# Two of the first query/key loads wait for a used buffer, and three more loads change places in the queue

## Chip, cores and metric

One NeuronCore of a Trainium2 chip (trn2). The time is that of one execution on the device, in microseconds (us); of several executions the median is given.

## What is computed

Attention with 4 batches, 8 heads, 576 positions and a head size of 64, in two parts that are added, followed by two mixer layers on the result. All data is float32 for q, k, v; the mixers' weights are 64-bit floats that the kernel itself converts.

```python
q_d, k_d, v_d = (t.reshape(B, H, Sd, 4, D).mean(axis=3) for t in (q, k, v))     # pooled by 4: 144 positions
out_up = np.repeat(sm_attn(q_d, k_d, v_d), 4, axis=2)                           # full softmax attention, repeated
mask = np.abs(pos[:, None] - pos[None, :]) < 4                                  # local: 7 neighbours
out_local = np.matmul(softmax(where(mask, q @ k.T / 8, -1e9)), v)
x = (out_up + out_local)                                                        # then as [B, S, 512]
u = x + (relu(x.T @ w_tok1) @ w_tok2).T;  x = u + relu(u @ w_ch1) @ w_ch2       # first mixer
th = x @ w_theta;  y = w_tok_r @ (x * cos(th)) + w_tok_i @ (x * sin(th))        # second mixer
u = x + y;  result = u + relu(u @ w_ch)
```

## The kernel before

The work is cut into small generators, one per step and tile, and a table `ORDER` (L33) lists by name which generator runs on next; each entry emits the instructions up to the generator's next `yield`. So the table sets the order of the instructions on every engine, and the engines then wait for one another by semaphores. What bears on the change lies in the first 100 us, the attention.

Heads are handled in 16 *pairs* (two heads of one batch; pairs 0 to 3 are batch 0, pairs 4 to 7 batch 1, and a tile `qk_1_3` is pair 7). For a pair n the steps are:

- `Pn` (`load_pair`, L375): one load of q and k of the pair, 128 partitions x 1164 values, 582 KB, into a tile `qk`. Four buffers exist; the pool gives each new tile one whose last reader is known.
- `Wn` (`load_values`, L382): four loads of the values `vw` (two of 32 rows, two of 6).
- `Kn` (`pool_pair`, L413): two additions on VectorE (L421, L422) that pool q and k by 4.
- `Ln` (`pair_local`, L522): local attention. 12 matmuls on zeros (24 for pair 0; L315) keep TensorE running, then the scores (L533, which read `qk`), a maximum and a subtraction on VectorE (L545, L546), the exponential on ScalarE (L553), transposes (L558), copies (L561), the product with `vw` (L568), and a division (L577 to L582). A pair's `qk` buffer is free when its L421 and its L533 have run.
- `An` (L590) adds the pooled part.

Two pairs make a quad Q. `VQ` (`pool_values`, L391) loads `vd` (650 KB) and pools it on GpSimd. `FQ` (`quad_front`, L425) is the pooled attention: scores (L434, L443), maxima (L452, L460), exponentials (L468, L473), transposes, the product `od` (L493 to L500), the division `ods` (L504 to L507), a store of `ods` to DRAM (L510, L511; the "store" below), and three loads `xu` of it, repeated (L516, L519; the "pooled loads"). `TQ`, `EQ`, `UQ` are the token mixer. `G0` to `G6` load and convert blocks of the token mixer's weights, `X0`, `X1`, ... those of the channel mixer: a load `raw` (L187), two operations on ScalarE (L199, L201), three on VectorE (L203, L206, L215), one on GpSimd (L219), a cast and a subtraction (L221, L223). `raw_2` and `raw_3` are blocks of `w_tok1` (512 KB), `raw_0`, `raw_4`, `raw_5` and `raw_6` of `w_tok2` (288 KB).

All these loads and stores are issued by SyncE (SP), one after the other in the order of the table; SP stops at one whose buffer is not free yet, and all behind it wait too. The framework gives the loads eight semaphores in turn (`DMAHW0` to `DMAHW7`), so that a load is also not issued before the load eight places ahead of it has landed.

The buffer of a pair's load, before:

```python
qk = sb2.tile([128, 2, S + 6], F32, tag="qk", name=f"qk_{b}_{p4}", bufs=4)   # L377
sp.dma_start(qk, qkT[b, p4])                                                 # L378
```

Of the kernel before, what the change touches and what calls it, by code (L numbers as in the profile page):

```python
# [12 lines left out]
F32 = mybir.dt.float32  # L13
# [101 lines left out]
def kernel(  # L115
# [172 lines left out]
    sb1 = actx.enter_context(tc.tile_pool(name="a1", bufs=1))  # L288
    sb2 = actx.enter_context(tc.tile_pool(name="a2", bufs=2))
# [3 lines left out]
    def wide(name):  # L293
        return big.tile([128, 2, 512], F32, tag="big", name=name)
# [25 lines left out]
    def step(name, gen):  # L320
        gens[name] = gen
# [200 lines left out]
    def pair_local(n):  # L522
# [426 lines left out]
    def lazily(f):  # L949
        yield from f()  # L950
# [190 lines left out]
    sb1 = ctx.enter_context(tc.tile_pool(name="c1p", reuse_waits="tile", bufs=1))  # L1141
    sb2 = ctx.enter_context(tc.tile_pool(name="c2p", reuse_waits="tile", bufs=2))
# [93 lines left out]
    T0, T1 = slice(0, HALF), slice(HALF, S)  # L1236
# [221 lines left out]
```

## Time and profile before

| | before |
|---|---|
| median of 3 runs | 682.81 us (680.63 to 683.04) |
| profiled execution | 679.18 us, its span 677.4 us |
| TensorE (PE) busy | 655.6 us, 97% |
| weight loads (PEld) busy | 625.6 us, 92% |
| VectorE (DVE) busy | 519.8 us, 77% |
| ScalarE (ACT) busy | 321.1 us, 47% |
| GpSimd (POOL) busy | 100.1 us, 15% |
| bytes moved by DMA | 109.93 MB, mean 162 GB/s |

The profile is of one execution; its rows are times in us from the start of the span. Busy shares are averages over stages with different limits. A row of a timeline names the engine, the source line, the operation, the tile written and the tiles read; in brackets stands how long the engine had been idle before it and what it waited for.

### The profile page before, as it was taken

What the parts mean: (1) busy time and instruction counts of PE and PEld (TensorE: products, weight loads), DVE (VectorE), ACT (ScalarE), POOL (GpSimd) and SP (SyncE); (2) the same over time, 40 slices, a digit from 0 to 9 for tenths busy, and PEclk for the clock granted to TensorE, in tenths of its full rate; (3) what the DMA queues carried; (4) which work ended last, traced back from release to release, by engine and by line L of the source; (5) the groups of instructions that cost most, each with busy time, mean ns of one, the idle gap of its engine ahead of it and who ended that gap; (6) DMA issues with size and microseconds to landing.
All of it is one profiled execution on the core that took longest, in us unless ns stands there. A gap on an engine that the chain in (4) does not pass through costs nothing.

```text
span 677.4 us, 17394 instructions
## 1 busy us (share of the span) xinstructions
PE 655.6 (97%) x7320; PEld 625.6 (92%) x7320; DVE 519.8 (77%) x952; ACT 321.1 (47%) x632; POOL 100.1 (15%) x92
## 2 busy tenths in 40 slices
PE   7779889999999999999999999999999999999997
PEld 4658879989999999999999999999999998998997
DVE  5989988697542888998987867677898748847837
ACT  3566758355342564535434523154647227427311
POOL 3224222415000423300101200012000000000000
PEclk8889999999999999999999999999999999999999
DMA  8797877757343685527263762699510330140202
GB/s 294 235 300 236 269 248 250 254 184 233 105 147 126 221 294 187 202 65 214 57 195 128 206 142 85 236 323 277 141 63 0 106 121 1 62 142 1 71 1 70
DMA packets 93021, 109.93 MB, mean 162 GB/s; under 512 B 46880, under 2 KB 69536, under 8 KB 92944
## 3 DMA queue, kind: packets, MB, share of 16 engines
q1 hardware_dynamic: 92080, 106.08, 49.4%
q0 software_dynamic: 864, 2.75, 1.1%
q8 instruction: 57, 0.93, 0.6%
q14 instruction: 20, 0.16, 0.1%
HBM read 79.13 MB, written 29.69 MB: 161 GB/s over the span
## 4 chain that ended last, share of the span: by engine, by line
PE 84%; DMA 5%; DVE 5%; SPq 2%; ACT 2%; issue 1%; DVEq 0%; ACTq 0%
PE y L157 6%; PE y L158 6%; PE y L159 6%; PE c L158 4%; PE c L157 4%; PE c L159 4%; PE c L699 4%; PE c L702 4%; PE c L700 4%; PE c_p L902 3%; PE c_p L905 3%; PE c_p L903 3%; PE th L158 2%; PE th L159 2%; PE th L157 2%; DMA qk<-qkT 2%
## 5 line engine op out<-in xcount | busy, mean ns | idle before, releaser
L158 PE MATMUL y<-wrl,zh 128*128 128x288 f32 x256 | 74.9, 296 | 0.0
L157 PE MATMUL y<-wrh,zh 128*128 128x288 f32 x256 | 74.8, 296 | 0.0
L159 PE MATMUL y<-wrh,zl 128*128 128x288 f32 x256 | 71.9, 295 | 0.0
L219 POOL TENSOR_TENSOR ww<-ww,raw 128x512 int32<-128x512 int32 (+2 forms) x30 | 41.0, 1373 | 160.1 <-DMA raw<-w_ch 52.9
L157 PEld LDWEIGHTS y<-wrh,zh 128*128 128x128 f32 x256 | 48.0, 188 | 0.0
L158 PEld LDWEIGHTS y<-wrl,zh 128*128 128x128 f32 x256 | 48.0, 188 | 0.0
L159 PEld LDWEIGHTS y<-wrh,zl 128*128 128x128 f32 x256 | 46.9, 188 | 0.0
L219 POOL TENSOR_TENSOR raw<-raw 128x512 int32<-128x512 int32 (+2 forms) x16 | 20.4, 1275 | 133.5 <-DVE raw L215 57.6
L1231 DVE TENSOR_TENSOR cx<-y,cx 128x288 f32<-128x288 f32 x32 | 14.6, 456 | 32.3 <-PE y L159 31.8
L151 ACT CAST cuh<-cx 128x288 fp32r<-128x288 f32 (+1 forms) x16 | 8.8, 553 | 59.6 <-DVE cx L1231 59.6
L199 ACT ACTIVATE ww<-raw 128x512 f32<-128x512 f32 (+2 forms) x30 | 19.5, 649 | 27.4 <-DVE c1l L223 9.5
L157 PE MATMUL th<-thh,cxh 128*128 128x512 f32 (+1 forms) x92 | 31.6, 343 | 0.0
L158 PE MATMUL th<-thl,cxh 128*128 128x512 f32 (+1 forms) x92 | 31.6, 343 | 0.0
L159 PE MATMUL th<-thh,cxl 128*128 128x512 f32 (+1 forms) x92 | 31.1, 343 | 0.0
L921 DVE SCALAR_TENSOR_TENSOR g<-c,g 128x384 fp32r<-128x384 f32 x40 | 21.1, 549 | 12.8 <-ACT g L918 12.8
L918 ACT ACTIVATE g<-c 128x384 fp32r<-128x384 f32 x40 | 19.2, 490 | 24.4 <-PE c L159 24.4
L201 ACT ACTIVATE raw<-raw 128x512 int32<-128x512 uint32 (+3 forms) x46 | 29.5, 641 | 0.0
L929 DVE TENSOR_TENSOR ut<-c,ut 128x384 f32<-128x384 f32 x32 | 17.1, 550 | 9.9 <-PE c L702 9.9
L568 PE MATMUL o<-vw,plt 38*32 38x65 f32 x1280 | 18.0, 231 | 3.8 <-issue 3.1
L157 PE MATMUL t<-w2h,h 128*128 128x256 f32 (+1 forms) x64 | 21.5, 337 | 0.0
L157 PE MATMUL c<-uh,c1h 128*128 128x384 f32 x64 | 21.4, 334 | 0.0
L159 PE MATMUL c<-uh,c1l 128*128 128x384 f32 x64 | 21.4, 334 | 0.0
(390 smaller groups left out, 2256.7 us busy)
## 6 DMA issues: line engine op xcount, KB each, us to landing
raw<-w_ch SPq DMA_DIRECT2D x27, 512.0 KB
qk<-qkT SPq DMA_DIRECT2D x16, 582.0 KB
xT<-ut SPq DMA_DIRECT2D x12, 768.0 KB
vd<-vtok SPq DMA_DIRECT2D x8, 650.0 KB
vw<-vloc SPq DMA_DIRECT2D x32, 146.2 KB
uT<-us SPq DMA_DIRECT2D x16, 288.0 KB
ut<-uT SPq DMA_DIRECT2D x6, 768.0 KB
ut<-xT SPq DMA_DIRECT2D x6, 768.0 KB
```

The lines of the kernel that those rows point to most:

```text
L157: pe.matmul(out, lh, rh, start=start, stop=False, skip_group_check=again)
L158: pe.matmul(out, lh, rl, start=False, stop=False, skip_group_check=again)
L159: pe.matmul(out, ll, rh, start=False, stop=stop, skip_group_check=again)
L201: act.activation(f, words[:, :, 0], AF.Copy, scale=2.0**-29)
L219: pool.tensor_tensor(out=w.bitcast(I32), in0=w.bitcast(I32), in1=f, op=ALU.add)
L699: pe.matmul(ps[:, 0:MIX], h[:, cb % 2, d], h1, start=cb == cbs[0], stop=False)
L700: pe.matmul(ps[:, 0:MIX], l[:, cb % 2, d], h1, start=False, stop=False)
L702: pe.matmul(ps[:, 0:MIX], weight[cb // 2][2][:, cb % 2, d], h2, start=False, stop=cb == cbs[-1])
L902: pe.matmul(ps[:, 0:MIX], h[:, cb % 2, d], h1, start=cb == cbs[0], stop=False)
L903: pe.matmul(ps[:, 0:MIX], l[:, cb % 2, d], h1, start=False, stop=False)
L905: pe.matmul(ps[:, 0:MIX], weight[cb // 2][2][:, cb % 2, d], h2, start=False, stop=cb == cbs[-1])
L921: dve.scalar_tensor_tensor(out=h2, in0=ps, scalar=0.0, in1=h1.bitcast(F32), op0=ALU.max, op1=ALU.subtract)
```

## The change

The table of the order is rewritten in its first four lines, and the buffer of each pair's load is set by hand.

```diff
 ORDER = """
-G3 P0 G2 I*2 P1 G3 P4 G3 V0 P2 G3 K0 G3 G2 I G2 I L0*2 P3 K1 F0 W1 L0 F0 L1 L0 G3 F0 V0 L1*2 V0 L2 W0 G1 G0 G6 V1 G2
-K2 V0 G2 F0 L1 F0 L2 K3 K4 L0 F0 L0 L2 L1 G2 F1 L2 L1 L0 F0 F1 G1*2 F1 V1 F0 P5 F0 W3 L0 F1 G5 G0 L1 G0 F1 K5 G6 F2 L1
...
+G3 P0 G2 I*2 P1 G3*2 V0 G3 K0 G3 G2 I G2 I L0*2 P2 W0 G1 K1 F0 L0 F0 L1 L0 G3 F0 V0 L1 P3 G0 W1 L1 V0 L2 G2 K2 V0 G2
+F0 G1 L1 F0 L2 G1 K3 L0 F0 L0 L2 F1 L1 G2 L2 L1 L0 F0 F1*2 F0 V1 P4 P5 F0 V1 G6 W3 L0 F1 G5 G0 L1 G0 F1 K4 K5 G6 F2 L1
...
+QK = (0, 1, 0, 1, 2, 3, 0, 1, 3, 2, 3, 0, 2, 1, 3, 0)
...
-        qk = sb2.tile([128, 2, S + 6], F32, tag="qk", name=f"qk_{b}_{p4}", bufs=4)
+        qk = sb1.tile([128, 2, S + 6], F32, tag=f"qk{QK[n]}", name=f"qk_{b}_{p4}")
```

Pair 2 now loads into pair 0's buffer and pair 3 into pair 1's; pairs 4 and 5 have buffers of their own and are loaded behind the first store; from pair 6 on each load takes the buffer of the same earlier pair as before. The added line moves the line numbers of the changed kernel up by one. The amount of work and the number of instructions stay the same; TensorE's order changes in one place (the scores of quad 1's second half, L434 and L443, now come before the transposes of pair 1, L558), and behind about 60 us all engines have the order of before.

SP, the first loads. The names are `qk` of a batch and pair, `vd` of a batch and quad, `vw` values, `raw` weights; in brackets the semaphores that the load waits for. Before:

```order
L378 DMA qk_0_1_148<-qkT 128x1164
L378 DMA qk_1_0_152<-qkT 128x1164
L396 DMA vd_0_0_157<-vtok 128x1300
L378 DMA qk_0_2_159<-qkT 128x1164 [waits DMAHW0_49]
L378 DMA qk_0_3_240<-qkT 128x1164 [waits DMAHW1_49,DVE_49,PE_49]
L387 DMA vw_0_1_266<-vloc 32x1170 [waits DMAHW2_49]
```

Now:

```order
L379 DMA qk_0_1_148<-qkT 128x1164
L397 DMA vd_0_0_155<-vtok 128x1300
L379 DMA qk_0_2_236<-qkT 128x1164 [waits DMAHW1_49,DVE_49,PE_49]
L388 DMA vw_0_0_238<-vloc 32x1170 [waits DMAHW0_49]
L388 DMA vw_0_0_238<-vloc 32x1170
L388 DMA vw_0_0_238<-vloc 6x1170 [waits DMAHW2_49]
L388 DMA vw_0_0_238<-vloc 6x1170 [waits DMAHW3_49]
L188 DMA raw_2_243<-w_tok1 128x2x256 [waits DMAHW4_49]
L379 DMA qk_0_3_342<-qkT 128x1164 [waits DMAHW5_49,DVE_49,PE_49]
```

Pair 4 (`qk_1_0`) is gone from the head of the queue, pair 2 stands where pair 3 stood and waits for the same readers of pair 0, and pair 3 has moved behind `vw_0_0` and `raw_2` and waits for the readers of pair 1.

SP, around the first store (`od`, `ot`) and the pooled loads (`xu`). Before:

```order
L187 DMA raw_4_373<-w_tok2 128x288 [waits DMAHW4_49]
L396 DMA vd_0_1_375<-vtok 128x1300 [waits DMAHW5_49,Pool_49]
L510 DMA od_0_0_57<-ods_0_0_567 4x32x256 [waits DMAHW6_49,DVE_49]
L511 DMA ot_0_0_65<-ods_0_0_567 4x32x64 [waits DMAHW7_49]
L378 DMA qk_1_1_589<-qkT 128x1164 [waits DMAHW0_49,PE_49]
L516 DMA xu_0_0_591<-od_0_0_57 128x1x1024 [waits DMAHW6_49,DMAHW1_49]
L519 DMA xu_0_0_591<-ot_0_0_65 64x1x256 [waits DMAHW7_49,DMAHW2_49]
L519 DMA xu_0_0_591<-ot_0_0_65 64x1x256 [waits DMAHW3_49]
L387 DMA vw_0_3_595<-vloc 32x1170 [waits DMAHW4_49,PE_49]
```

Now:

```order
L511 DMA od_0_0_57<-ods_0_0_562 4x32x256 [waits DMAHW3_49,DVE_49]
L512 DMA ot_0_0_65<-ods_0_0_562 4x32x64 [waits DMAHW4_49]
L397 DMA vd_0_1_578<-vtok 128x1300 [waits DMAHW5_49,Pool_49]
L379 DMA qk_1_0_580<-qkT 128x1164 [waits DMAHW6_49]
L379 DMA qk_1_1_582<-qkT 128x1164 [waits DMAHW7_49]
L517 DMA xu_0_0_584<-od_0_0_57 128x1x1024 [waits DMAHW3_49,DMAHW0_49]
L520 DMA xu_0_0_584<-ot_0_0_65 64x1x256 [waits DMAHW4_49,DMAHW1_49]
L520 DMA xu_0_0_584<-ot_0_0_65 64x1x256 [waits DMAHW2_49]
L188 DMA raw_4_589<-w_tok2 128x288
L388 DMA vw_0_3_591<-vloc 32x1170 [waits PE_49]
```

`vd_0_1` and `raw_4` were issued ahead of the store and now come behind it, and both pairs 4 and 5 stand between the store and the pooled loads. Further on, at the second store (`od_0_1`), pair 7's load moves in the same way: it stood ahead of the store and stands behind the three `xu` loads of it now, and so does `vd_1_0`; the weights `raw_7` and `raw_8` of the channel mixer swap places.

DVE, the pooling of pairs 2 to 4 (`qa`, `qkd`), the conversion of `raw_2`, and the maximum of pair 2 (`mx_0_2`). Before:

```order
L546 TENSOR_TENSOR pbuf1_120<-s_0_1_278,mx_0_1_344 128x2x5x38
L421 TENSOR_TENSOR qa_0_2_379<-qk_0_2_159 128x576
L422 TENSOR_TENSOR qkd_0_1_378<-qa_0_2_379 128x288
L421 TENSOR_TENSOR qa_0_3_443<-qk_0_3_240 128x576
L422 TENSOR_TENSOR qkd_0_1_378<-qa_0_3_443 128x288
L421 TENSOR_TENSOR qa_1_0_447<-qk_1_0_152 128x576
L422 TENSOR_TENSOR qkd_1_0_446<-qa_1_0_447 128x288
L545 TENSOR_REDUCE mx_0_2_488<-s_0_2_349 128x10
```

Now:

```order
L547 TENSOR_TENSOR pbuf1_120<-s_0_1_276,mx_0_1_351 128x2x5x38
L422 TENSOR_TENSOR qa_0_2_373<-qk_0_2_236 128x576
L423 TENSOR_TENSOR qkd_0_1_372<-qa_0_2_373 128x288
L204 TENSOR_SCALAR raw_2_243<-raw_2_243 128x512
L207 TENSOR_SCALAR raw_2_243<-raw_2_243 128x512
L216 SCALAR_TENSOR_TENSOR raw_2_243<-raw_2_243 128x512
L422 TENSOR_TENSOR qa_0_3_442<-qk_0_3_342 128x576
L423 TENSOR_TENSOR qkd_0_1_372<-qa_0_3_442 128x288
L546 TENSOR_REDUCE mx_0_2_483<-s_0_2_356 128x10
```

The conversion of `raw_2` stood seven places behind `mx_0_2` and now stands ahead of pair 3's pooling; pair 4's pooling has left this place for one behind `raw_3`'s conversion, just ahead of pair 5's.

## Rows read from the trace of the kernel before

**Rows 1.** Busy time by stretches of the span; the first line names the columns.
```profile
core 0: us, PE busy (x) PEld busy (x) DVE busy (x) ACT busy (x) POOL busy (x), PEclk, DMA share, GB/s
0.00:9.54 9.54, 6.48 (x126) 4.06 (x126) 3.71 (x10) 3.44 (x7) 2.56 (x8) 1.00 0.81 279
10.90:14.10 3.20, 3.20 (x29) 1.78 (x29) 2.87 (x6) 1.17 (x4) 1.41 (x2) 0.50 1.10 393
...
19.00:24.00 5.00, 4.70 (x201) 3.77 (x187) 3.96 (x11) 3.45 (x9) 0.00 (x0) 1.00 1.02 371
24.00:35.09 11.09, 7.92 (x254) 5.72 (x252) 10.62 (x23) 5.63 (x16) 5.95 (x6) 0.85 0.66 215
...
38.00:45.00 7.00, 3.64 (x170) 2.89 (x172) 6.11 (x11) 6.20 (x14) 0.00 (x0) 1.00 0.89 297
100.00:160.00 60.00, 59.00 (x1108) 54.08 (x1109) 50.58 (x94) 37.17 (x88) 17.20 (x20) 1.00 0.70 229
```

**Rows 2.** Chain that ended last, in order of time: start, us, what.
```profile
3.53 5.99 DMA qk<-qkT
...
42.99 1.85 issue
...
127.51 7.42 DMA qk<-qkT
```

**Rows 3.** Timeline of VectorE: start, us, line, tiles, count, [idle before, releaser].
```profile
5.63 1.19 DVE L421 TENSOR_TENSOR qa<-qk 128x576 f32<-128x576 f32 x1 [0.37 <-DMA qk<-qkT]
...
7.88 0.43 DVE L215 SCALAR_TENSOR_TENSOR raw<-raw 128x256 uint32<-128x256 uint32 x1
...
15.92 0.55 DVE L545 TENSOR_REDUCE mx<-s 128x10 f32<-128x380 f32 x1 [1.65 <-PE s L533]
...
19.54 0.76 DVE L421 TENSOR_TENSOR qa<-qk 128x576 f32<-128x576 f32 x1
...
20.71 0.55 DVE L545 TENSOR_REDUCE mx<-s 128x10 f32<-128x380 f32 x1
...
25.15 0.43 DVE L203 TENSOR_SCALAR raw<-raw 128x512 f32<-128x512 f32 x1
...
26.07 0.69 DVE L215 SCALAR_TENSOR_TENSOR raw<-raw 128x512 uint32<-128x512 uint32 x1
...
48.52 0.83 DVE L421 TENSOR_TENSOR qa<-qk 128x576 f32<-128x576 f32 x1
```

**Rows 4.** Timeline of ScalarE, the conversion of raw_5.
```profile
35.09 0.48 ACT L199 ACTIVATE ww<-raw 128x288 f32<-128x288 f32 x1 [4.25 <-DMA raw<-w_tok]
```

**Rows 5.** Timeline of SP, the issuing queue.
```profile
1.20 0.42 SPq L378 DMA_DIRECT2D qk<-qkT  x1
...
8.81 0.33 SPq L378 DMA_DIRECT2D qk<-qkT  x1
...
24.41 0.44 SPq L378 DMA_DIRECT2D qk<-qkT  x1
...
43.53 0.60 SPq L516 DMA_DIRECT2D xu<-od  x1
```

**Rows 6.** Timeline of TensorE, the matmuls on zeros of pairs 1 and 2.
```profile
11.99 2.89 PE L315 MATMUL s<-zero 128*128 128x320 bf16 x12
...
15.82 1.80 PE L315 MATMUL s<-zero 128*128 128x320 bf16 x12
```

**Rows 7.** DMA issues: tiles, queue, count, KB of each.
```profile
qk<-qkT SPq DMA_DIRECT2D x16, 582.0 KB
...
vd<-vtok SPq DMA_DIRECT2D x8, 650.0 KB
vw<-vloc SPq DMA_DIRECT2D x32, 146.2 KB
...
xu<-od SPq DMA_DIRECT2D x8, 512.0 KB
...
raw<-w_tok SPq DMA_DIRECT2D x4, 288.0 KB
```

More of the change, by code (lines that the diff above doesn't have):

```diff
@@ L33 @@
 ORDER = """
-G3 P0 G2 I*2 P1 G3 P4 G3 V0 P2 G3 K0 G3 G2 I G2 I L0*2 P3 K1 F0 W1 L0 F0 L1 L0 G3 F0 V0 L1*2 V0 L2 W0 G1 G0 G6 V1 G2
-K2 V0 G2 F0 L1 F0 L2 K3 K4 L0 F0 L0 L2 L1 G2 F1 L2 L1 L0 F0 F1 G1*2 F1 V1 F0 P5 F0 W3 L0 F1 G5 G0 L1 G0 F1 K5 G6 F2 L1
-G0 P6 W2 G5 G6 L3 V1 F2 V1 L3 G6 F2 F1 L3 G1 G4 F1 L2 P7 L5 L2 L5 F1 G1 L3 A0 V2 X0 A1 T0 L3 G1 L5 G0 L3 T0 G0 L2 G2
-F1 G4 F2 G5 T0 K6 T0 V2 X2 L2 G6 W5 F2 K7 V2 L4*2 E0.0*2 T0 L4 V3 V2 A2 L3 E0.1 L5 G4 L4 W4 L5 G6 L5 G4 L3 X2 F3 G5 P8
+G3 P0 G2 I*2 P1 G3*2 V0 G3 K0 G3 G2 I G2 I L0*2 P2 W0 G1 K1 F0 L0 F0 L1 L0 G3 F0 V0 L1 P3 G0 W1 L1 V0 L2 G2 K2 V0 G2
+F0 G1 L1 F0 L2 G1 K3 L0 F0 L0 L2 F1 L1 G2 L2 L1 L0 F0 F1*2 F0 V1 P4 P5 F0 V1 G6 W3 L0 F1 G5 G0 L1 G0 F1 K4 K5 G6 F2 L1
+G0 P6 W2 G5 G6 L3 V1 F2 V1 L3 G6 F2 F1 L3 G1 G4 F1 L2 L5 L2 L5 F1 G1 L3 A0 A1 T0 L3 G1 L5 G0 L3 T0 G0 L2 G2 F1 P7 V2
+G4 F2 G5 T0 K6 T0 V2 X2 L2 G6 W5 F2 K7 V2 L4*2 E0.0*2 T0 L4 V3 V2 A2 L3 E0.1 L5 G4 L4 X0 W4 L5 G6 L5 G4 L3 X2 F3 G5 P8
 P9 A3 G4 F2 G5 E0.1 T1 G4 G5 T0 F2 V3 L4 F3 F2 T0 L4 V3 X2 F3 L6 V3 L6 X7 T0 P11 L6 X2 X0 F3 K8 U0.0 L6 T0 X2 X0 U0.0
```

## The prediction

> **What bounds the kernel now.** I read four views, from coarse to fine.
>
> First the busy time by stretches. From 100 to 160 us TensorE is busy 59.0 of 60 us [rows 1]; it runs its instructions in a fixed order there, so what the front part of the program gains or loses reaches the end of the span nearly one to one. Ahead of that TensorE is not full: 7.92 of 11.09 us from 24 to 35.09, 3.64 of 7 us from 38 to 45 [rows 1]. VectorE is: 10.62 of 11.09 us between 24 and 35.09 [rows 1]. So the change is worth what it does to the first 50 us, where VectorE's queue and the landings of loads take turns at setting the pace.
>
> Second the chain that ended last. It runs through the landing of pair 1's q and k (5.99 us from issue, so at 9.5 us), and later through two stretches called "issue", one of them 1.85 us at 42.99 [rows 2]: TensorE waits there for nothing that the profile shows.
>
> Third the timelines. VectorE starts pair 1's maximum at 15.92 after 1.65 us without work, and comes to pair 2's maximum at 20.71, having pooled pairs 2, 3 and 4 in between [rows 3]. ScalarE stands still for 4.25 us until `raw_5` lands at 35.09 [rows 4]; everything behind that on ScalarE, the exponentials of quad 2 among it, starts from there. Pair 3's load leaves at 8.81, when the readers of pair 0 are through [rows 5].
>
> Fourth the transfers: 279 GB/s up to 9.54 us, 371 from 19 to 24, but only 215 between 24 and 35.09 [rows 1], where SP waits for the store and for landings.
>
> **The change part by part.** I count the delay, in us, at two points of the program that both executions pass: pair 2's maximum on VectorE, and the landing of `raw_5`.
>
> *Pairs 4 and 2 leave the head of the queue.* Pair 1 landed at 9.5 us, when 279 GB/s x 9.54 us = 2660 kB had been moved. What is issued up to pair 1, by the list of issues and the two small loads behind pair 0, is about 1.9 MB, so some 0.8 MB of the loads behind it (pair 4, `vd`, pair 2) had got ahead of it. With only `vd` behind it pair 1 can land earlier. VectorE cannot use that before `raw_1` is done, at 7.88 + 0.43 = 8.31 [rows 3]. The gain lies between 0 (they move strictly in the order of issue) and 1.2 us; I take the middle, -0.6. The Trainium skill's page "DMA: Bandwidth & Descriptors" says in "Queues, rings and completion order" that each DMA engine takes descriptors in ring order; by that alone the later loads would not delay pair 1, this term would be 0 and the sum +0.7. The count of bytes speaks against taking it so strictly, and so I keep the half.
>
> The twelve matmuls on zeros of pair 1 took 2.89 us and those of pair 2, at the other clock level, 1.80 [rows 6]; from 10.9 to 14.1 the granted clock was 0.50, that is 1.2 instead of 2.4 GHz [rows 1]. Right ahead of the fall TensorE had waited for pair 1's pooling. A shorter wait may spare the fall, worth 0 to -1.1. The same kinds of instruction stand there, so I take 0.
>
> *Pair 2 now waits for pair 0's readers.* It is issued at 8.81 as pair 3 was. Pair 0, with only `raw_0` ahead of it, took from 1.20 to 5.63, 4.4 us [rows 3, 5]; with 5 us pair 2 lands at about 13.8. VectorE needs it at 15.92 - 0.6 + 1.1 = 16.4. Covered by 2.6 us; without the cover it would cost one for one.
>
> *Pair 3 now waits for pair 1's readers.* These end when pair 1's maximum can start, 15.92 - 0.6 = 15.3. The queue is nearly drained then, but `raw_3` and `vw_0_1` are issued right behind. Its flight is bounded by 4.4 us (pair 0) and 7.42 us (a pair's load at 127.51 [rows 2]); I take 5.0, nearer to pair 0, and so 20.3. VectorE has, from 15.3, the maximum and subtraction (1.1), pair 2's pooling (20.71 - 19.54 = 1.2 for one pair) and the three conversions of `raw_2` (26.07 + 0.69 - 25.15 = 1.6) [rows 3]: it is ready at 19.2 and waits 1.1, say +1.0 (0.4 to 3.4 by the two ends). Queued behind that wait is pair 2's maximum, then the division that feeds the first store.
>
> *`raw_2` goes ahead of pair 2's maximum, pair 4's pooling behind it.* 1.6 us in, 1.2 us out: in the sum of VectorE nothing, at this one point it is already in the line above (ready at 19.2 + 1.2 for pair 3, against 20.71: -0.3 without the wait). I count 0; by 36 us both have been done.
>
> *`vd_0_1`, pairs 4 and 5 and `raw_4` stand between the store and `raw_5`.* SP reaches `vd_0_1` where pair 5 was issued, 24.41 [rows 5], plus the delay so far. To move up to and with `raw_5`: 650 + 2 x 582 + 512 + 2 x 288 + 2 x 146 = 3194 KB [rows 7], 3270 kB, and at the 371 GB/s of a full queue [rows 1] 8.8 us. The fixed part of a load's flight is, from pair 0 with `raw_0` ahead of it, 4.4 - (582 + 288) KB at that rate (2.4) = 2.0. So 24.41 + 2.0 + 8.8 = 35.2 instead of 35.09, and the small pieces that I left out (tails, store) make it some tenths later: +0.3. Ends: -0.6 if the store lands sooner on an emptier queue and lets SP go on, +1.5 if the pooled loads are held behind the two pairs, since the `raw_5` load waits for the `xu` load eight places ahead. ScalarE's 4.25 us of idle time hide `raw_4`'s later landing; `vd_0_1` is needed by GpSimd, which has slack of some 2 us there.
>
> *Pair 7, `vd_1_0` and `raw_7` leave the stretch ahead of the second store.* From 38 to 45 us 297 GB/s x 7 us = 2080 kB move [rows 1]; 582 + 650 KB, 1260 kB, of that go later. The 1.85 us of "issue" at 42.99 [rows 2] stand amid full transfers. If TensorE waits there for its own instructions, which also come by DMA, an emptier queue shortens it: 0 to -1.85; I take a third, -0.6. Pair 7 itself is issued behind the three `xu` loads, at 43.53 + 2 = 45.5 at the latest [rows 5], lands 4.4 to 5 us later, and VectorE wants it at 48.52 [rows 3]: 0 to +2. With the sooner store it is there in time; I take 0. The swap of `raw_7` and `raw_8` and the buffers' new places move no one on the path: 0.
>
> **Sum.** -0.6 + 1.0 + 0.3 - 0.6 = +0.1 us. Against the profiled execution 679.18 + 0.1 = 679.3; the median shown is 682.81, 3.6 above that execution, so the median I expect is **682.9 us**: no change. About 0.5% (3.4 us) is what a measurement of this kernel can tell from no change.
>
> **Rivals.**
> - *The front gains.* Pair 1 lands 1.2 sooner, the clock does not fall (-1.1), the "issue" stretch goes (-1.85), pair 3 flies 4.4 us (+0.4), `raw_5` comes 0.6 sooner: -4.4, 678.4 us. For it: 0.8 MB ahead of pair 1, and the idle time on SP between 24 and 35 us. Against it: all must come together.
> - *Pair 3's late load becomes the bound.* Pair 1 gains nothing, its readers end at 15.9, pair 3 flies 7.42 us to 23.3, VectorE was ready at 19.8: +3.4, and `raw_5` another +0.6: +4.0, 686.8 us. It decides from a flight of about 4 us on; every us above that is lost on VectorE, which has no spare time until 35 us. Against it: the queue has drained when pair 3 is issued. The same skill page, under "Rules for kernel authors", asks to issue a DMA early and to wait for it late; the change does the opposite with pairs 2, 3 and 4, and by that rule it would end here. No row shows that early loads were free: pair 4 rode beside pair 1 and was wanted by VectorE at 19.54 only [rows 3].
> - *The change doesn't do what it says for the time:* what the first 25 us gain or lose is made up by the next wait (`raw_5` at 35.09 lands when the bytes are through, whoever was issued first): 0, 682.8 us.
>
> **How the numbers follow.** Forecast (within 2 us of no change) 0.50, the third rival 0.15, the gain 0.20, the loss 0.15. The gain and the loss cross the bound in most but not all of their weight, and the forecast's far ends add a little: faster 0.17, within 0.5% 0.70, slower 0.13. The bounds of all terms together span -4.4 to +6.9; leaving out one in ten on each side, 679.2 to 686.3 us.
>
> **What would show it.** In the changed profile: pair 1's pooling starts at 8.3 to 9.5; pair 3's pooling on VectorE waits about 1 us for its load; the granted clock between 11 and 14 us; ScalarE's wait for `raw_5` ends at 34.5 to 36.5; the "issue" stretch at 43 us; pair 7's pooling without a wait. TensorE from 100 to 160 as full as before. The prediction is wrong if VectorE at 60 us stands more than 3.4 us from where it stood, or if a wait appears that I put at 0.

## The result, and the profile after

| | before | changed |
|---|---|---|
| median | 682.54 us (680.63 to 684.48, 10 runs) | 686.74 us (684.34 to 692.06, 10 runs) |
| ratio | | 1.0071, 95% interval 1.0051 to 1.009 |
| profiled execution | 679.18 us, span 677.4 | 687.14 us, span 685.3 |
| PE, PEld, DVE busy | 655.6, 625.6, 519.8 us | 659.6, 627.6, 521.0 us |
| bytes moved | 109.93 MB | 109.93 MB |

The changed kernel is slower by 0.7%, by the ratio 4.8 us; the forecast was 682.9 us, no change, in a range up to 686.3. The execution of before whose rows stand above the prediction was a quick one. The kernel before was therefore profiled once more (e0 below): span 681.5 us. Rows of after are set against both.

Busy time of the changed kernel in the stretches of [rows 1]:

```profile
core 0: us, PE busy (x) PEld busy (x) DVE busy (x) ACT busy (x) POOL busy (x), PEclk, DMA share, GB/s
0.00:9.54 9.54, 7.08 (x126) 4.26 (x126) 3.47 (x9) 3.49 (x7) 2.56 (x8) 1.00 0.77 262
10.90:14.10 3.20, 2.75 (x28) 1.62 (x29) 2.73 (x6) 1.34 (x5) 2.73 (x3) 0.69 0.94 285
19.00:24.00 5.00, 4.71 (x200) 3.74 (x201) 4.71 (x12) 2.24 (x5) 0.00 (x0) 1.00 0.72 214
24.00:35.09 11.09, 4.97 (x198) 3.69 (x201) 6.83 (x12) 4.92 (x13) 4.46 (x4) 0.89 0.83 283
...
100.00:160.00 60.00, 58.15 (x1282) 52.68 (x1281) 49.02 (x92) 34.62 (x80) 13.99 (x14) 1.00 0.73 237
```

From 19 to 24 us 214 GB/s move, where 371 did; from 24 to 35.09 it is 283 instead of 215 [rows 1]. The transfers have been pushed behind the store. And VectorE, which was busy for 10.62 of 11.09 us in that stretch, is now busy for 6.83: it waits. TensorE from 100 to 160 us is about as full as before: 58.15 of 60, against 59.00 [rows 1] and 58.10 in e0.

The chain that ended last, of the changed kernel (start, us, what):

```profile
3.52 6.11 DMA qk<-qkT
...
12.08 3.38 PE s L316 x12
...
25.77 6.20 DMA qk<-qkT
31.99 1.76 DVE qa L422
33.78 0.91 DVE qkd L423
34.71 1.07 DVE qa L422
...
37.54 2.69 PE s L316 x12
...
43.60 1.35 issue
...
48.93 4.74 DMA qk<-qkT
```

Two new loads stand in it: pair 4's, 6.20 us from its issue at 25.77, and pair 7's, 4.74 us. Behind pair 4's come its pooling, pair 5's, quad 2's scores and pair 3's zeros, all in one row. An "issue" stretch of 1.35 us stands at 43.60, but it is not the one of [rows 2], as the rows of TensorE below show.

VectorE's timeline of the changed kernel (columns as in [rows 3]):

```profile
9.65 0.76 DVE L422 TENSOR_TENSOR qa<-qk 128x576 f32<-128x576 f32 x1 [1.23 <-DMA qk<-qkT]
...
16.59 0.56 DVE L546 TENSOR_REDUCE mx<-s 128x10 f32<-128x380 f32 x1 [2.82 <-PE s L534]
...
20.43 0.76 DVE L422 TENSOR_TENSOR qa<-qk 128x576 f32<-128x576 f32 x1
...
21.60 0.55 DVE L546 TENSOR_REDUCE mx<-s 128x10 f32<-128x380 f32 x1
...
27.90 0.17 DVE L578 TENSOR_SCALAR rl<-o 128x10 f32<-128x10 f32 x1 [2.75 <-PE o L569]
...
31.99 1.75 DVE L422 TENSOR_TENSOR qa<-qk 128x576 f32<-128x576 f32 x1 [1.29 <-DMA qk<-qkT]
33.78 0.90 DVE L423 TENSOR_TENSOR qkd<-qa 128x288 f32<-128x288 f32 x1
34.71 1.06 DVE L422 TENSOR_TENSOR qa<-qk 128x576 f32<-128x576 f32 x1
...
41.27 0.55 DVE L546 TENSOR_REDUCE mx<-s 128x10 f32<-128x380 f32 x1 [1.28 <-PE s L534]
...
50.02 0.75 DVE L422 TENSOR_TENSOR qa<-qk 128x576 f32<-128x576 f32 x1
...
53.69 0.76 DVE L422 TENSOR_TENSOR qa<-qk 128x576 f32<-128x576 f32 x1 [1.25 <-DMA qk<-qkT]
...
57.32 0.86 DVE L204 TENSOR_SCALAR raw<-raw 128x288 f32<-128x288 f32 x1
...
68.83 0.96 DVE L422 TENSOR_TENSOR qa<-qk 128x576 f32<-128x576 f32 x1
```

Read it from the top. Pair 1's pooling starts at 9.65, as late as before. Pair 3's (20.43) does not wait. Pair 2's maximum (21.60) is 0.9 us behind [rows 3], and level with e0's (21.77). Then comes a wait of 2.75 us for TensorE ahead of pair 0's division (27.90): before, `raw_2`'s conversion was done in that wait (26.07 [rows 3]), and now it has been done already. Pair 4's pooling waits 1.29 us for its load and takes 1.75 us where 0.76 is usual. Pair 7's waits 1.25 us (53.69). The last line (68.83) is pair 8's pooling.

SP's timeline of the changed kernel:

```profile
9.08 0.33 SPq L379 DMA_DIRECT2D qk<-qkT  x1
...
16.58 0.36 SPq L379 DMA_DIRECT2D qk<-qkT  x1
...
25.77 0.90 SPq L379 DMA_DIRECT2D qk<-qkT  x2
```

ScalarE's, the conversions of `raw_4` and `raw_5`:

```profile
37.15 0.46 ACT L200 ACTIVATE ww<-raw 128x288 f32<-128x288 f32 x1 [6.99 <-DMA raw<-w_tok]
...
39.43 0.47 ACT L200 ACTIVATE ww<-raw 128x288 f32<-128x288 f32 x1 [1.46 <-DMA raw<-w_tok]
```

GpSimd's, the pooling of `vd_0_1` and `vd_1_0`:

```profile
30.55 1.34 POOL L399 TENSOR_TENSOR vd<-vd 128x650 f32<-128x650 f32 x1 [15.61 <-DMA vd<-vtok]
31.86 1.27 POOL L220 TENSOR_TENSOR raw<-raw 128x512 int32<-128x512 int32 x1
...
55.38 1.33 POOL L399 TENSOR_TENSOR vd<-vd 128x650 f32<-128x650 f32 x1 [14.39 <-DMA vd<-vtok]
```

TensorE's, the second half of pair 1's product, and two later stops:

```profile
32.99 0.90 PE L569 MATMUL o<-vw,plt 38*32 38x65 f32 x40 [2.95 <-issue]
...
44.95 0.75 PE L534 MATMUL s<-qk 64*32 64x38 f32 x62 [1.35 <-issue]
...
48.74 0.42 PE L569 MATMUL o<-vw,plt 38*32 38x65 f32 x20 [0.74 <-issue]
```

And the stop of [rows 2], in TensorE's timeline of the kernel before:

```profile
44.84 0.57 PE L568 MATMUL o<-vw,plt 38*32 38x65 f32 x20 [1.85 <-issue]
```

Pair 3's load leaves at 16.58 instead of 8.81 [rows 5], pairs 4 and 5 at 25.77. `raw_4` lands at 37.15 and `raw_5` at 39.43; the latter was 35.09 [rows 4]. GpSimd pools `vd_0_1` from 30.55, just ahead of pair 4's pooling on VectorE, and `vd_1_0` from 55.38. TensorE has an "issue" stop of 2.95 us amid the late transfers; it is not in the chain, which runs through pair 4's load there. The stop of [rows 2] stands ahead of the last 20 matmuls of a product (1.85 us); at the same place after has 0.74 us, and its 1.35 us stand at another, inside a pair's scores, where before had 0.81. In e0 neither place has a stop.

### The profile page after: what moved, and what is told of

Same layout as the page of the kernel before. It is cut to its first block, busy times and chain, and to the rows that moved or that the text cites. A ratio compares the mean times of both kernels' runs of the same rounds, so it can differ in the third digit from the quotient of the medians.

```text
span 685.3 us, 17388 instructions
## 1 busy us (share of the span) xinstructions
PE 659.6 (96%) x7320; PEld 627.6 (92%) x7320; DVE 521.0 (76%) x952; ACT 321.2 (47%) x632; POOL 98.1 (14%) x92
## 2 busy tenths in 40 slices
DMA packets 93022, 109.93 MB, mean 160 GB/s; under 512 B 46881, under 2 KB 69537, under 8 KB 92945
## 3 DMA queue, kind: packets, MB, share of 16 engines
q0 software_dynamic: 864, 2.75, 1.0%
## 4 chain that ended last, share of the span: by engine, by line
PE 83%; DMA 7%; DVE 6%; ACT 2%; SPq 1%; issue 1%; DVEq 0%; ACTq 0%
PE y L159 6%; PE y L158 6%; PE y L160 6%; PE c L158 4%; PE c L159 4%; DMA qk<-qkT 4%; PE c L160 4%; PE c L700 4%; PE c L703 4%; PE c L701 4%; PE c_p L904 3%; PE c_p L906 3%; PE c_p L903 3%; PE th L159 2%; PE th L160 2%; PE th L158 2%
## 5 line engine op out<-in xcount | busy, mean ns | idle before, releaser
L569 PEld LDWEIGHTS o<-vw,plt 38*32 38x32 f32 x1280 | 15.0, 106 | 9.7 <-issue 6.0
```

Of the source, the lines that this page charges most:

```text
L569: pe.matmul(o[r : r + 32, 5 * j + i // 2], pts[h : h + W, i // 2, r : r + 32], vw[h : h + W, g, :], start=True, stop=True,)
```

## The experiments

Every kernel was run beside the kernel before on the same chip. The edits are all in the table of the order (and one in the number of zeros). A diff shows only the pieces that differ; "-" is the changed kernel, or before, as said.

**e0: the kernel before, once more.**

> The kernel before, unchanged, for a second profile: every theory expects the same chain in the first 60 us, with ScalarE's wait for raw_5 ending at 35 us plus or minus 1, and the place of the later stages within 2 us. If it stands 3 us or more later behind 60 us, the first profile was a quick execution, and part of the 7.9 us between the two profiles is that.

683.33 us, span 681.5. VectorE there comes to pair 3's maximum at 39.95, not 35.83 as in the first profile; by then the changed kernel is 1.3 us behind. Its timeline of VectorE, with the last piece of `raw_2`'s conversion, pair 0's division, and the pooling of pairs 6 (48.36) and 8 (66.38):

```profile
27.13 1.82 DVE L215 SCALAR_TENSOR_TENSOR raw<-raw 128x512 uint32<-128x512 uint32 x1
28.98 0.17 DVE L577 TENSOR_SCALAR rl<-o 128x10 f32<-128x10 f32 x1
...
39.95 0.55 DVE L545 TENSOR_REDUCE mx<-s 128x10 f32<-128x380 f32 x1 [2.54 <-PE s L533]
...
48.36 1.89 DVE L421 TENSOR_TENSOR qa<-qk 128x576 f32<-128x576 f32 x1
...
66.38 0.97 DVE L421 TENSOR_TENSOR qa<-qk 128x576 f32<-128x576 f32 x1
```

Two executions of one kernel are thus 4 us apart, as much as the change costs. No single profile gives its price; only the ratios do.

**e1: the loads back ahead of the first store** (changed kernel).

```diff
-P3 G0 W1 L1 V0 L2
+P3 G0 W1 L1 V0 G6 V1 P4 L2
-F0 V1 P4 P5 F0 V1 G6 W3
+F0 P5 F0 V1 W3
```

> The changed kernel with one thing undone: raw_4, vd_0_1 and pair 4 are issued behind vw_0_1 again, ahead of the first store; pairs 2 and 3 still load into used buffers, pair 7 stays behind the second store. Theory A (the queue behind the first store): these loads meet an idle queue there, ScalarE's wait for raw_5 ends 3 us or more sooner than in the changed kernel (at 36.5 us or before, against 39.4), VectorE does not wait for pair 4, and the time falls by 2.5 to 4.5 us to a ratio of 0.999 to 1.003 against the kernel before. Theory B (the late loads of pairs 2 and 3 at the start): it falls by less than 1 us, ratio 1.005 to 1.008. Theory C (pair 7 behind the second store): likewise less than 1 us, and VectorE's wait before pair 7's pooling stays.

Ratio 1.0063 (1.0034 to 1.0092). `raw_5` lands at 35.81, 3.6 us sooner, and pair 4 no longer keeps its pooling waiting, but the time stays, as far as the interval tells. The queue behind the store is not the loss by itself.

**e2: pair 7 and `vd_1_0` back ahead of the second store's pooled loads** (changed kernel).

```diff
-F1 L2 L5 L2 L5 F1 G1 L3 A0 A1 T0
+F1 L2 P7 L5 L2 L5 F1 G1 L3 A0 V2 A1 T0
-L2 G2 F1 P7 V2
+L2 G2 F1
```

> The changed kernel with pair 7 and vd_1_0 put back ahead of the pooled loads of the second store (pair 7 ahead of the store itself). Theory C: the wait of 1.25 us on VectorE before pair 7's pooling goes and the time falls by 1.2 to 2.5 us, ratio 1.003 to 1.005. Theories A and B: by less than 1 us, ratio 1.006 to 1.008; the landing of raw_5 stays at about 39 us.

1.0069 (1.0039 to 1.01). Pair 7's wait is gone; pair 4's is longer in this execution, 3.24 us.

**e3: `vd_0_1` and `raw_4` alone late** (on before).

```diff
-W0 G1 G0 G6 V1 G2
+W0 G1 G0 G2
-F1 V1 F0 P5 F0 W3
+F1 F0 V1 P5 F0 V1 G6 W3
```

> The kernel before with one part of the change: vd_0_1 and raw_4 are issued behind the first store (raw_4 behind its pooled loads); pairs 2, 3, 4, 5 and 7 as before. Theory A: with pair 4 not in that stretch the bytes are 596 kB fewer than in the changed kernel, so raw_5 lands 1 to 2.5 us later than before (36 to 37.6) and the time rises by 1 to 3 us, ratio 1.001 to 1.004. Theories B and C: within 0.5 us of the kernel before, ratio 0.999 to 1.001.

1.0029 (1.0 to 1.0058). Pair 5's pooling waits 1.58 us and is then stretched beside GpSimd.

**e4 and e5: pair 4's pooling into the wait ahead of pair 0's division.** e4 is e1 with this; e5 is e4 with e2's edit too. Against e1:

```diff
-L0 F0 F1*2 F0 P5 F0 V1 W3
+L0 F0 F1*2 K4 F0 P5 F0 V1 W3
-F1 K4 K5 G6
+F1 K5 G6
```

> The changed kernel with raw_4, vd_0_1 and pair 4 issued ahead of the first store (as in e1_ahead) and pair 4's pooling moved on VectorE into the wait ahead of the division of pair 0. Theory D (pair 4's pooling has come onto the path that leads through pair 5's pooling, quad 2's scores and pair 3's maximum): the wait ahead of that division shrinks by 1.2 us, pair 5's pooling starts 1.2 to 2.2 us sooner than in e1_ahead, and the time falls by 1 to 2.5 us from e1_ahead, ratio 1.002 to 1.005. Rival (the stretch is set by TensorE's stops in the product of pair 0 and by its clock): no gain, 1.0055 to 1.0075.

> As e4_k4_hole, and pair 7 and vd_1_0 back ahead of the pooled loads of the second store: of the change only the used buffers of pairs 2 and 3, the conversion of raw_2 ahead of pair 2's maximum, and the swapped weights are left. Theories A, C and D together: 1 to 2 us below e4_k4_hole, ratio 0.999 to 1.003. If the late loads of pairs 2 and 3 are what costs (theory B): 1.004 or more.

e4: 1.0042 (1.0013 to 1.0072); e5: 1.0018 (0.999 to 1.0045). With all but the front undone (the used buffers, `raw_2` ahead, `raw_7` and `raw_8` swapped) the loss is down to what can't be told from none. But in e5 VectorE waits 3.63 us for pair 3 and 1.54 for pair 4: a wait for a load is not by itself a loss of that size. VectorE of e5:

```profile
22.20 0.76 DVE L422 TENSOR_TENSOR qa<-qk 128x576 f32<-128x576 f32 x1 [3.63 <-DMA qk<-qkT]
...
28.47 0.76 DVE L422 TENSOR_TENSOR qa<-qk 128x576 f32<-128x576 f32 x1 [1.54 <-DMA qk<-qkT]
```

**e6: pair 4's pooling alone late. e7: pair 7 and `vd_1_0` alone late** (each on before).

```diff
-L2 K3 K4 L0
+L2 K3 L0
-F1 K5 G6 F2 L1
+F1 K4 K5 G6 F2 L1
```

```diff
-F1 L2 P7 L5 L2 L5 F1 G1 L3 A0 V2 X0 A1
+F1 L2 L5 L2 L5 F1 G1 L3 A0 X0 A1
-F1 G4 F2
+F1 P7 V2 G4 F2
```

> The kernel before with pair 4's pooling alone moved on VectorE to just ahead of pair 5's; all loads as before. Theory D: pair 2's maximum comes 1.2 us sooner, pair 5's pooling ends 0.5 to 1.5 us later, and the time rises by 0.5 to 2 us, ratio 1.001 to 1.003. Rival (VectorE's sum alone counts): no change, 0.999 to 1.001.

> The kernel before with pair 7 and vd_1_0 issued behind the second store's pooled loads, nothing else. Theory C as a part of the loss: pair 7's pooling waits 0.5 to 2 us for its load, and the time rises by 0.5 to 2 us, ratio 1.001 to 1.003. If it is covered: 0.999 to 1.001.

e6: 1.0028 (1.0001 to 1.0056); e7: 1.0008 (0.9988 to 1.0028).

**e8 and e9: without pair 3's twelve matmuls on zeros** (before, and the changed kernel). These zeros stood on the path in e0 (3.38 us) and in after (2.69 in its chain).

```diff
-WARM = [24] + [12] * 3 + [0] * 12
+WARM = [24] + [12] * 2 + [0] * 13
```

> The kernel before, with the twelve matmuls on zeros of pair 3 left out and nothing else (they add nothing to the result). Theory (these zeros stand on the path: in the executions so far they took 1.8 us at 2.4 GHz and 3.4 us at 1.2 GHz, ahead of pair 3's scores, on which VectorE waited 0.6 to 2.5 us): ratio 0.997 to 0.999, mx_3 starts 1 to 3 us sooner. Rival (the clock stays at the low level for longer without them, so that the scores and transposes behind pay it back, or raw_5's landing is what counts): ratio 0.999 to 1.004.

> The changed kernel with the same twelve matmuls left out. Theory (in the changed kernel pair 4's pooling, pair 5's pooling, quad 2's first scores, these zeros and pair 3's scores stand in one row, so the zeros' 1.8 to 3.4 us are on the path): ratio 1.003 to 1.006, against 1.007 with them. Rival (the clock stays low for longer, or the late landings behind the store set the pace alone): 1.006 to 1.010.

e8: 1.0037 (1.0017 to 1.0056), a loss; e9: 1.0081 (1.0049 to 1.0113). The rivals' ratios came out: nothing is won by leaving them out, in either kernel. Which of their reasons holds is not shown.

**e10: the changed kernel, a second profile.**

> The changed kernel once more, for a second profile. If the reading of the first one holds, VectorE waits again 1 to 1.5 us for pair 4's load ahead of its pooling, pair 7's pooling waits again about 1.2 us, mx_3 starts at 40 to 42 us, and the span is 682 to 686 us. If these waits were chance, at least one of them is gone with the span about as long.

686.52 us, span 684.7. Its timeline of VectorE:

```profile
8.60 0.76 DVE L422 TENSOR_TENSOR qa<-qk 128x576 f32<-128x576 f32 x1
...
13.88 0.55 DVE L546 TENSOR_REDUCE mx<-s 128x10 f32<-128x380 f32 x1 [1.12 <-PE s L534]
...
19.66 0.77 DVE L422 TENSOR_TENSOR qa<-qk 128x576 f32<-128x576 f32 x1 [1.05 <-DMA qk<-qkT]
```

Here the granted clock was 1.00 from 10 to 24 us, and pair 1's maximum came 2.7 us sooner than in after. Most of it was given back: VectorE waited 1.05 us for pair 3, 1.84 for pair 4 and 2.26 for pair 7, and the span is 0.6 us shorter than in after. The waits for pairs 4 and 7 are there again; a gain ahead of them ends in them.

With two profiles of each kernel it can be read where the loss stands. The rows give the start on VectorE, in us:

| | before | e0 | after | e10 | mean difference |
|---|---|---|---|---|---|
| pair 1's maximum | 15.92 | 16.97 | 16.59 | 13.88 | -1.2 |
| pair 3's maximum | 35.83 | 39.95 | 41.27 | 40.23 | +2.9 |
| pair 8's pooling | 62.97 | 66.38 | 68.83 | 69.48 | +4.5 |
| pair 15's pooling | 134.96 | 138.81 | 142.61 | 142.02 | +5.4 |
| span | 677.4 | 681.5 | 685.3 | 684.7 | +5.5 |

About half of the difference is there by pair 3's maximum, most of the rest comes between it and pair 8's pooling, where pair 7's wait stands, and next to nothing behind pair 15's. Against e0 alone pair 3's maximum is only 0.3 to 1.3 us late, so the size of the first half is not settled by these profiles.

**e11: the three single edits of e3, e6 and e7 together** (on before).

> The kernel before with the three single edits together: vd_0_1 and raw_4 behind the first store, pair 4's pooling behind raw_3's conversion just ahead of pair 5's, pair 7 and vd_1_0 behind the second store. Pairs 2, 3 and 4 are loaded where and into what they were before. Theory (the loss is made behind the first store, of parts that add up, and the late loads of pairs 2 and 3 cost nothing): ratio 1.005 to 1.008, as the changed kernel. Rival 1 (the late loads of pairs 2, 3 and 4 make a third or more of it): 1.001 to 1.004. Rival 2 (the parts hide one another): about 1.003, that of the dearest alone.

1.0019 (0.9995 to 1.0044). Neither the sum of the parts (1.0065) nor the loss of the change. What was missing was pair 4's late load, the front, or both.

**e12: e11 and pair 4's load late too** (the first diff, against e11). **e13: the front alone**, that is the changed kernel with all else undone, but for the swap of `raw_7` and `raw_8`.

```diff
-P1 G3 P4 G3 V0 P2
+P1 G3*2 V0 P2
-F0 V1 P5 F0 V1 G6 W3
+F0 V1 P4 P5 F0 V1 G6 W3
```

```diff
-P1 G3*2 V0 G3
+P1 G3 P4 G3 V0 G3
-P3 G0 W1 L1 V0 L2
+P3 G0 W1 L1 V0 G6 V1 L2
-K3 L0 F0
+K3 K4 L0 F0
-F0 V1 P4 P5 F0 V1 G6 W3
+F0 P5 F0 V1 W3
-F1 K4 K5 G6
+F1 K5 G6
...
```

(The second diff is e13's, against the changed kernel; e2's edit belongs to it too.)

> The kernel before with the three edits of e11_three_late and, fourth, pair 4's load moved from the head of the queue to its place in the changed kernel, between vd_0_1 and pair 5 behind the first store; pairs 2 and 3 stay early, in buffers of their own. Theory (pair 4's late load is what is missing: its pooling stands on the row to quad 2's scores and waits for it, and its 582 KB are ahead of raw_4 and raw_5): pair 4's pooling waits 1 us or more, raw_5's conversion starts at 38 to 40 us, ratio 1.005 to 1.008. Rival (the used buffers of pairs 2 and 3 make the rest): ratio 1.001 to 1.004, as without it.

> The changed kernel with all that it does behind the first store undone: pair 4's load back at the head of the queue and its pooling behind pair 3's, vd_0_1 and raw_4 ahead of the store, pair 7 and vd_1_0 ahead of the second store's pooled loads. What is left of the change: pairs 2 and 3 into the buffers of pairs 0 and 1, the places of vw_0_0 and raw_2 in the queue, raw_2's conversion ahead of pair 3's pooling, raw_7 and raw_8 swapped. Theory (this part costs nothing that can be measured): ratio 0.998 to 1.003. Rival (it makes the missing half per cent: pair 3's load is late, raw_2's conversion no longer fills VectorE's wait ahead of pair 0's division): 1.003 to 1.007, with a wait of 1 us or more ahead of pair 3's pooling.

e12: 1.0082 (1.0051 to 1.0113); e13: 1.002 (0.9992 to 1.0048). The late load of pair 4 turns e11's small loss into that of the change, and VectorE of e12 shows it:

```profile
33.47 0.90 DVE L421 TENSOR_TENSOR qa<-qk 128x576 f32<-128x576 f32 x1 [2.86 <-DMA qk<-qkT]
```

e13 has no wait for a load of pairs 2 to 7. What its profile does show is the wait that `raw_2` no longer fills; but e13's ratio can't be told from 1, so no price of it is shown. VectorE of e13:

```profile
29.27 0.17 DVE L578 TENSOR_SCALAR rl<-o 128x10 f32<-128x10 f32 x1 [2.93 <-PE o L569]
```

**e14: the changed kernel with pair 4's load alone back at the head. e15: pair 4's load and pooling alone late** (on before).

```diff
-P1 G3*2 V0 G3
+P1 G3 P4 G3 V0 G3
-F0 V1 P4 P5 F0 V1 G6 W3
+F0 V1 P5 F0 V1 G6 W3
```

```diff
-P1 G3 P4 G3 V0 P2
+P1 G3*2 V0 P2
-F1 V1 F0 P5 F0 W3
+F1 V1 F0 P4 P5 F0 W3
-L2 K3 K4 L0
+L2 K3 L0
-F1 K5 G6 F2 L1
+F1 K4 K5 G6 F2 L1
```

> The changed kernel with one thing undone: pair 4 is loaded at the head of the queue, as before (into its own buffer; its pooling stays just ahead of pair 5's). vd_0_1, raw_4, pair 7 and vd_1_0 stay late. Theory (pair 4's late load makes most of the loss): no wait ahead of pair 4's pooling, ratio 1.001 to 1.004. Rival (the loss is that of any 3.2 MB rearranged behind the store, or of the front): 1.006 to 1.009, as the changed kernel.

> The kernel before with pair 4 alone late: its load between the first store and pair 5's, its pooling just ahead of pair 5's. vd_0_1 and raw_4 stay ahead of the store, pair 7 ahead of the second. Theory A (pair 4's load is enough): its pooling waits over 1 us, ratio 1.004 to 1.008. Theory B (it needs the 938 KB of vd_0_1 and raw_4 in the same stretch to become late): it is there in time or nearly, ratio 1.002 to 1.004, as the pooling's move alone (1.0028).

e14: 1.0066 (1.0039 to 1.0093); e15: 1.0055 (1.0026 to 1.0083). So my theory fell in one direction and held in the other: pair 4's load and pooling late make a loss of that order alone, but with the load early and all else as changed the loss stays. In the profile of e15 the pooling does not wait for the load (31.71, no wait), so a wait there isn't what its loss comes from. In e14 pair 4's pooling starts at 29.53 with no wait, and runs into GpSimd instead, which works from 29.92 to 34.97 us there. VectorE of e14:

```profile
29.53 0.75 DVE L422 TENSOR_TENSOR qa<-qk 128x576 f32<-128x576 f32 x1
30.32 1.48 DVE L423 TENSOR_TENSOR qkd<-qa 128x288 f32<-128x288 f32 x1
31.83 1.73 DVE L422 TENSOR_TENSOR qa<-qk 128x576 f32<-128x576 f32 x1
```

**e16: e14 with pair 4's pooling early too. e17: e13 with pair 4's pooling late.** The edit is e6's, on those two, taken back in e16 and made in e17.

> The changed kernel with pair 4 back at both its places: loaded at the head of the queue and pooled behind pair 3. Used buffers for pairs 2 and 3, vd_0_1, raw_4, pair 7 and vd_1_0 stay as the change has them. Theory (the late place of pair 4's pooling is the necessary part): ratio 1.001 to 1.004, against 1.0066 with the pooling late. Rival (the late loads behind the stores add up whatever VectorE does): 1.005 to 1.008.

> The kernel of e13_used_buffers with one more edit, pair 4's pooling moved behind raw_3's conversion, ahead of pair 5's; all loads behind the first store as before. Theory (raw_2's conversion moved forward and pair 4's pooling moved back are one exchange: together they leave VectorE empty ahead of pair 0's division and put 1.2 us behind it): VectorE waits 1.5 to 3 us for TensorE ahead of the division, ratio 1.004 to 1.007. Rival (without the late loads it is hidden): 1.001 to 1.003.

e16: 1.0086 (1.0054 to 1.0118); e17: 1.0044 (1.0023 to 1.0065). The late place of pair 4's pooling is not needed either. With pair 4 out of it, e16 waits for pair 5 and pair 7. VectorE of e16:

```profile
32.56 1.36 DVE L422 TENSOR_TENSOR qa<-qk 128x576 f32<-128x576 f32 x1 [1.89 <-DMA qk<-qkT]
...
54.06 0.76 DVE L422 TENSOR_TENSOR qa<-qk 128x576 f32<-128x576 f32 x1 [2.27 <-DMA qk<-qkT]
```

**All of them together.** The change has five parts: F (the front: used buffers for pairs 2 and 3, `raw_2` ahead, `raw_7` and `raw_8` swapped), P (pair 4's load behind the store), K (its pooling late), V (`vd_0_1`, `raw_4` late), S (pair 7, `vd_1_0` late).

| kernel | parts in it | ratio - 1, % | VectorE waits for pairs 2 to 7, us |
|---|---|---|---|
| changed (two profiles) | F P K V S | 0.71 | 2.54, 5.15 |
| e16 | F V S | 0.86 | 4.40 |
| e12 | P K V S | 0.82 | 5.34 |
| e2 | F P K V | 0.69 | 5.31 |
| e14 | F K V S | 0.66 | 2.14 |
| e1 | F K S | 0.63 | 2.64 |
| e15 | P K | 0.55 | 0 |
| e17 | F K | 0.44 | 0.35 |
| e4 | F S | 0.42 | 5.66 |
| e3 | V | 0.29 | 1.58 |
| e6 | K | 0.28 | 0 |
| e13 | F | 0.20 | 0 |
| e11 | K V S | 0.19 | 2.66 |
| e5 | F | 0.18 | 5.17 |
| e7 | S | 0.08 | 0.17 |

(In e1, e4 and e5 pair 4's load stands ahead of the store and is not counted as late, nor is e4's and e5's pooling of it in the idle time.) One fixed price for each part, fitted to these fifteen ratios with their intervals as weights, gives F 0.25 (error 0.06), P 0.21 (0.09), K 0.16 (0.07), V 0.13 (0.08), S 0.11 (0.07) per cent. The sum is 0.86, against 0.71 measured. The fit is rough: e16 lies 0.37 above its sum, e11 0.21 below, more than their intervals allow for easily. One and the same price for every part, 0.17, fits nearly as well, so the five prices are not told apart, and those of V and S lie within two errors of nothing. What is shown is less: **no single part makes the whole loss, and leaving out F, P or S does not take it away.** One part alone costs 0.08 to 0.29, two 0.42 to 0.55, three or four 0.63 to 0.86 (but e11, three parts, 0.19). Without F (e12), without P (e14) and without S (e2) the loss is still 0.66 to 0.82.

What stays open is the price of a single part: each, alone, is within or close to what a measurement can tell. That the waits for loads are what all have in common can't be said: each of the kernels above 0.6 waits over 2 us for loads of pairs 2 to 7, and e4 and e5 wait as long and lose less, while e15 waits for none and loses 0.55. No version was faster than before; e5, e7, e11 and e13 can't be told from it.

One thing was not varied: the granted clock of TensorE. Averaged over its runs, each kernel of the table that was run with recorded clocks of before beside it had a lower one than before, by 0.001 to 0.006 of full speed, but for e7. A mean lower by 0.0025 is 3.4 us more at 1.2 GHz in 685 us, in which a busy TensorE gets 1.7 us less done (an estimate from these clocks). Whether the lower clock is a cause of the loss or comes from the waits, no run shows.

## Why the prediction was wrong

Terms that were put at or near zero were not, and two gains did not come. How the parts make up the 0.71% together stays open.

- **The step that failed first: "in the sum of VectorE nothing", with +1.0 for pair 3 as the whole price of the front and of pair 4's pooling.** e17, which is these two alone (F and K), measured 1.0044, 3.0 us (1.6 to 4.4). That they cost more than was counted is shown; why is argued. `raw_2` forward and pair 4's pooling back were counted as an exchange of 1.6 against 1.2 us. Such an exchange need not be neutral when one side has idle time and the other not: in before `raw_2`'s conversion ended right ahead of pair 0's division, where after has 2.75 us of idle time (27.90), and pair 4's pooling came to stand in the one row that leads to pair 3's maximum. Against this reading stands e0: there the last piece of that conversion took 1.82 us, and the division came at 28.98, later than in after.
- **No term for pair 4's load.** The text asked when VectorE needs pairs 2, 3 and 7; of pair 4 it didn't ask. Its flight was 6.20 us from 25.77, and its pooling waited 1.29 us (1.84 in e10). Added to e11, the late load takes the ratio from 1.0019 to 1.0082, 4.3 us, where the sum had -0.6 for its leaving the head of the queue and +0.3 for the loads behind the store. But taken out of the change it gives nothing back that can be told (e14, 1.0066).
- **"+0.3" for the loads between the store and `raw_5`.** The landing of `raw_5` was worked out as 35.2; it was 39.43 (37.74 in e10). The sum of bytes was taken at the rate of a full queue, 8.8 us. From 24 to 35.09 the queue moved 283 GB/s, not 371, and SP issued `raw_5`'s load at 35.41, where before it was at 32.42: it had waited 1.3 us for a pair's load to land, ahead of the values, and 1.5 us for the first pooled load, ahead of `raw_5`'s own. The text names that last wait and ends at +1.5; the landing came 4.3 us later than before (2.7 in e10). But this delay is not the loss by itself either, as e1 shows, with `raw_5` at 35.81 and 1.0063.
- **Pair 7 "in time; I take 0".** It was issued at 48.93, not by 45.5, because the second store came later too, flew 4.74 us and was waited for, 1.25 us. That is the upper part of the 0 to +2 written there; alone (e7) it costs nothing that can be told.
- **Pair 3, "+1.0".** No wait in after, 1.05 us in e10. From its issue to its pooling it took at most 3.85 us in after and 5.8 in e10, but 7.7 in e5 (22.20, issued at 14.48): the bounds of 4.4 and 7.42 were both passed. The rival built on it ("pair 3's late load becomes the bound", 686.8 us) has the right sign; that its time is nearly the measured one is luck, since in after pair 3 keeps nothing waiting.
- **Pair 1, "-0.6".** In after itself nothing (9.65 against 9.54). Over the nine profiles with pair 4 out of the head, pair 1's pooling starts at 9.09 us on the mean; over the eleven with it there, at 9.40; single ones lie between 8.18 and 10.07. The difference, 0.3 us, is about the error of these means, so neither 0 nor the -0.6 is excluded by it. The rule of the Trainium skill ("DMA: Bandwidth & Descriptors", "Queues, rings and completion order"), that a ring is worked in order, gave 0. The traces agree with it within that difference.
- **"Issue", "-0.6".** A third of one stop, read from one execution. At its place the stop was 0.74 us in after instead of 1.85, but that of 0.81 us ahead of it became 1.35; e0, the same kernel as before, has neither. Such stops come and go between executions of one kernel, and no gain from fewer transfers is shown.
- Right were: pair 2 covered (17.65, no wait); next to no gain or loss behind 100 us, where TensorE is about as full as before; the third rival's working, that what the front gains ends in the next wait (e10, 2.7 us gained and most of it given back).

The sum by the fit: F and K 2.8 us, P and V 2.3, S 0.7, together 5.8, against 4.8 measured and +0.1 forecast. As the fit does not tell the parts apart, this is an account of the size and no proof of the shares.

The Trainium skill's page "DMA: Bandwidth & Descriptors", under "Rules for kernel authors", asks for DMAs to be issued early and waited for late. The runs do not go against it: the kernels with one group of loads moved back (e3, e7, e13) measured 0.29, 0.08 and 0.20% above before, the last two not told from zero. But e11, with 650 + 288 + 582 + 650 = 2170 KB issued later, is a loss that can't be told from zero either.

## What to carry to other kernels

- When loads are moved behind a wait of the issuing queue, ask for **each** of them when its reader comes to it, and not only for those that wait for a buffer; the landing must be worked out from the queue's rate with its stops (here 283 GB/s), not with the rate of a full queue (371).
- Work that is exchanged on an engine can have two prices, counted apart: one for the idle time it used to fill, one for the row it now stands in (here argued, not shown by a run of its own). Look at what ended the idle time ahead of the place it leaves and of the place it comes to.
- Where five small edits come in one, each below what can be measured, try several at a time, and in both directions, before one is named as the cause: "with it the loss comes" (e12) and "without it the loss goes" (e14) are two questions, and they had two answers here.

## What was unexpected of the hardware

**VectorE is slow beside GpSimd, and the slow stretch moves with the load.** The first addition of a pair's pooling takes 0.75 us; started while GpSimd works it takes 1.75 (31.99 in after; GpSimd's next operation, from 31.86, ends at 33.13) or 1.89 (48.36 in e0; GpSimd's ends at 49.63). In both it ends 0.6 us behind GpSimd's operation. GpSimd of e0:

```profile
48.19 1.44 POOL L398 TENSOR_TENSOR vd<-vd 128x650 f32<-128x650 f32 x1 [9.79 <-DMA vd<-vtok]
```

In the changed kernel `vd_1_0` comes at 55.38, pair 6's pooling (50.02) takes 0.75 us again, and now the conversion at 57.32 takes 0.86 instead of 0.30. So in these traces the later load did not make this cost; it picked who pays it. The Trainium skill ("Trainium Architecture — The Big Picture", "What this means for kernel authors") says that VectorE and GpSimd contend for a shared pair of ports to SBUF, under an exclusive lock; the rows agree, with 1.0 to 1.1 us more for one such instruction.

**The same order on the same chip scatters by more than the change costs.** The 29 executions of before beside e1, e2 and e3, on one chip, took 677.11 to 686.66 us. One place where profiles of one kernel differ is pair 3's zeros: they took 1.80 us in before, at a granted clock of 1.00 (2.4 GHz), and 3.38 us in e0, at 0.50 (1.2 GHz); [rows 6] show 1.80 and 2.89 for two other pairs. Leaving these zeros out did not win the time back (e8, e9).
